# Loading the first piece of a transposed input whole, and rotating a projection's output tiles through eight PSUM banks instead of four

## The chip, the core and the metric

The kernel runs on one core of a Trainium2 chip. The metric is the device time of one execution in microseconds (us), as the median of several runs. Everything said below of the hardware comes from the profile of one execution and its trace.

## The reference

Two attention blocks read the same input `x` (1 x 2048 x 1024, bf16) and a gate mixes their results. Block A is linear attention, block B a sliding, dilated window of 8 keys. Cut to what matters here:

```python
def _A_ref(x, wqkv, wo):
    # H = 32 heads of Dh = 32
    q, k, v = qkv[0], qkv[1], qkv[2]                 # of x @ wqkv
    phi = lambda t: jnp.where(t > 0, t + 1, jnp.exp(t)) + 1e-6
    pq, pk = phi(q), phi(k)
    kv = jnp.einsum("bhsd,bhse->bhde", pk, v)
    z = jnp.einsum("bhsd->bhd", pk)
    num = jnp.einsum("bhqd,bhde->bhqe", pq, kv)
    den = jnp.einsum("bhqd,bhd->bhq", pq, z)[..., None] + 1e-6
    return (num / den) @ wo

g = _sigmoid((x * gate_w).sum(-1, keepdims=True))
return g * _A_ref(...) + (1 - g) * _B_ref(...)       # B: softmax over 8 keys, dilation 2
```

The change lies in the first stage only, which computes `pk = phi(x @ Wk)` of block A.

## The kernel before

The kernel is one long sequence of matrix products on TensorE (PE), with the order of PE's instructions written out by hand. Its stages are: A's key projection (`pk`, line 159), the products `G = x^T pk` (line 209) with sums and the gate's dot products beside them, small per-head products, the projections of B's values and A's queries (lines 284 and 320), B's windowed attention (lines 377 and 434 to 457), and the output projections (line 575).

In the first stage `x` is cut into 16 tiles of 128 rows (`t` from 0 to 15) and the 1024 output columns into two halves of 512. One output tile is 128 x 512 in f32 and fills one PSUM bank; eight matmuls, one for each block `kt` of 128 input columns, add up in it. The stationary operand is a 128 x 128 block of `x` transposed (`xT`), which DMA transposes bring in from memory. These all go out from the queue of SyncE (SP), mixed with plain loads of the weights.

The stage starts before `x` is there. So the first eight row tiles of half 0 are computed with the loop over `kt` outside: in four phases `k` of two `kt` each, every phase needs a quarter of the weight half `WkA0` (line 98) and two transposed pieces of `x` (line 94), for rows 0 to 511 and rows 512 to 1023. In phase 0 alone the first of these two pieces is issued in two halves. The quarter of the weights for phase 0 goes out from the queue of ScalarE (ACT), everything else from SP. After these pieces SP issues the row tiles 8 to 15, one transpose each (line 104), then the second weight half `WkA1` and the loads for the later stages (lines 81 and 89). While the first piece is on its way, PE runs 38 small matmuls on a constant (`warm_up`, line 165).

The eight open output tiles of the first eight rows use all eight PSUM banks: tiles 0 to 3 the pool `ps_pj` (tag `pj`, four banks), tiles 4 to 7 the pool `ps_1` (tag `p1`, four banks). All later tiles (8 to 15 of half 0, then 0 to 15 of half 1) take `ps_pj` alone, in turn. A tile gets a bank when the bank's tile before it has been read for the last time.

The function `phi` empties a bank in three steps: ACT writes `e = exp(pj)` (line 145), VectorE (DVE) takes `min(e, 1) + 1e-6` (line 146), and DVE writes `pk = max(pj, 0) + e` (line 147), which is the last reader of the bank. DVE's order in this stage is written out too: it goes from tile to tile.

GpSimd (POOL) builds a mask for block B in the meantime, with 72 selects (line 125) that nothing in this stage needs.

Of the kernel before, what the change touches and what calls it, by code (L numbers as in the profile page):

```python
# [11 lines left out]
F32 = mybir.dt.float32  # L12
# [3 lines left out]
P = 128  # L16
# [23 lines left out]
def kernel(  # L40
# [18 lines left out]
    def rows(ap, s0, s1):  # L59
        return ap[s0 // 1024, s0 % 1024:(s1 - 1) % 1024 + 1, :]  # L60
# [13 lines left out]
    ps_pj = ctx.enter_context(tc.tile_pool(name="ps_pj", bufs=4, space=bass.MemoryType.PSUM))  # L74
# [18 lines left out]
    def load_xT(k, t0, t1):  # L93
        nc.sync.dma_start_transpose(out=xT[:, 2 * k:2 * k + 2, t0 * P:t1 * P],  # L94
                                    in_=rows(x, t0 * P, t1 * P)[:, 2 * k * P:(2 * k + 2) * P])

    for k in range(4):
        (nc.sync if k else nc.scalar).dma_start(  # L98
            out=WkA[0][:, 2 * k:2 * k + 2, :],
            in_=A_wqkv[2 * k * P:(2 * k + 2) * P, D:D + 512].rearrange("(kt p) n -> p kt n", p=P))  # L100
        for t0, t1 in ((0, 4), (4, 8)) if k else ((0, 2), (2, 4), (4, 8)):
            load_xT(k, t0, t1)
    for t in range(8, NB):
        nc.sync.dma_start_transpose(out=xT[:, :, t * P:(t + 1) * P], in_=rows(x, t * P, (t + 1) * P))
    WkA += load_w("WkA", A_wqkv, D, "wa", only=(1,))
# [37 lines left out]
    def phi(work, dst, pj):  # L143
        e = work.tile([P, 512], F32, name="e", tag="e")
        nc.scalar.activation(out=e[:], in_=pj[:], func=ACT.Exp)  # L145
        nc.vector.tensor_scalar(out=e[:], in0=e[:], scalar1=1.0, scalar2=1e-6, op0=ALU.min, op1=ALU.add)  # L146
        nc.vector.scalar_tensor_tensor(out=dst, in0=pj[:], scalar=0.0, in1=e[:], op0=ALU.max, op1=ALU.add)  # L147

    with tc.manual_schedule(engines={PE}):

        with ExitStack() as s1:
            ps_1 = s1.enter_context(tc.tile_pool(name="ps_1", bufs=4, space=bass.MemoryType.PSUM))
# [5 lines left out]
            def project(pj, t, kt, half):  # L158
                nc.tensor.matmul(pj[:], lhsT=xT[:, kt, t * P:(t + 1) * P], rhs=WkA[half][:, kt, :],  # L159
                                 start=(kt == 0), stop=(kt == KT - 1))  # L160

            def warm_up(n):
                warm = ps_1.tile([P, P], F32, name="warm", tag="p1")
                for i in range(n):
                    nc.tensor.matmul(warm[:], lhsT=onesb[:], rhs=onesb[:], start=True, stop=True)


            warm_up(38)
            first = [(ps_pj.tile([P, 512], F32, name="pk_ps", tag="pj") if t < 4 else
                      ps_1.tile([P, 512], F32, name="pk1_ps", tag="p1")) for t in range(8)]  # L170
            for k in range(4):
                for t in range(8):
                    for kt in (2 * k, 2 * k + 1):
# [3 lines left out]
            for half in range(2):  # L177
                for t in range(NB):
                    if half == 0 and t < 8:
                        continue  # L180
                    pj = ps_pj.tile([P, 512], F32, name="pk_ps", tag="pj")
                    for kt in range(KT):
                        project(pj, t, kt, half)
                    phi(work, pk[:, t, half * 512:(half + 1) * 512], pj)
# [18 lines left out]
            for half in range(2):  # L203
                g_ = junk.tile([P, KT, 512], BF16, name=f"G{half}", tag=f"G{half}")
                G.append(g_)
                for kt in range(KT):
                    pj = ps_pj.tile([P, 512], F32, name="g_ps", tag="pj")
# [142 lines left out]
        with ExitStack() as s2:  # L350
# [159 lines left out]
            for c in range(KT):  # L510
                kts[c] = kpool.tile([P, 2, 1024], BF16, name="kt", tag="kt")
                for hh in range(2):
# [3 lines left out]
                    if 1 <= c <= 2:  # L516
                        t = 2 * (c - 1) + hh
# [28 lines left out]
        with ExitStack() as s3:  # L546
# [15 lines left out]
            def out_part(i, tb, c0, n):  # L562

                st = {}

                def mm(side, c):
                    if side == 0 and c == 0:
                        st["ps"] = ps_3.tile([P, 512], F32, name="e3_ps", tag="p3") if i % 2 else \
                            ps_pj.tile([P, 512], F32, name="d3_ps", tag="pj")
                    if side == 0:  # L570
                        lhsT, W = (pqT[0][:, c, tb * P:(tb + 1) * P] if tb < 4 else
                                   pqT[1][:, c, (tb - 4) * P:(tb - 3) * P]), WoA
                    else:
                        lhsT, W = OBT[:, c, tb * P:(tb + 1) * P], WoB
                    nc.tensor.matmul(st["ps"][:, 0:n], lhsT=lhsT, rhs=W[c0 // 512][:, c, c0 % 512:c0 % 512 + n],  # L575
                                     start=(side == 0 and c == 0), stop=(side == 1 and c == KT - 1))
                    if side == 0 or c < KT - 1:
                        return
                    osb = work3.tile([P, 512], BF16, name="osb", tag="e")
                    nc.scalar.activation(out=osb[:, 0:n], in_=st["ps"][:, 0:n], func=ACT.Copy,  # L580
                                         scale=omg[:, tb:tb + 1])
                    nc.scalar.dma_start(out=rows(out2, tb * P, (tb + 1) * P)[:, c0:c0 + n], in_=osb[:, 0:n])

                def side(k):
                    for c in range(KT):
                        mm(k, c)
                return side
# [3 lines left out]
            first = [out_part(i, *p_) for i, p_ in enumerate(parts[:7])]  # L591
# [42 lines left out]
```

## Time and profile before

| | us |
|---|---|
| median of three runs | 478.88 (478.12 to 479.05) |
| profiled execution, its own time | 478.26 |
| its span, first to last instruction | 476.5 |
| PE busy in the span | 468.6 (98%) |
| DVE busy | 278.2 (58%) |
| ACT busy | 168.6 (35%) |
| matmuls of the first stage (line 159), 256 of them | 56.6 busy, 3.8 idle before them |

An engine's busy time is the time in which it had an instruction at work. A line of the profile names source line, engine, operation, and the tiles written and read. "Idle before" is the time in which the engine had nothing to do just before an instruction of that group, and the arrow names what ended the wait. The operations on SP are the issues of DMAs: their time is that of the issue, not of the transfer. The granted clock of PE was 1.00 in all slices of the span.

### The profile page before, as it was taken

The page shows a single profiled execution, that of the slowest core. Times are in us where ns is not written, and L with a number is a line of the kernel's source. Part 1 is how long each engine was busy: PE and PEld are TensorE (multiplying, and loading weights), DVE is VectorE, ACT ScalarE, POOL GpSimd, SP SyncE. Part 2 cuts the span into 40 slices and gives each one's busy share as a digit, 9 for nine tenths or more (in the row PEclk, how much of TensorE's full clock was granted, in tenths as well). Part 3 has the DMA queues.
Part 4 walks back from the last instruction along what each step waited for, and adds up shares of the span by engine and source line. Part 5 has one row for each costly group of instructions (what it writes and reads, how often), then busy time and mean ns, then how long its engine had stood idle before and what let it go on. Part 6 is the DMA issues. An engine that isn't in the chain of part 4 may idle for free.

```text
span 476.5 us, 13198 instructions
## 1 busy us (share of the span) xinstructions
PE 468.6 (98%) x5750; PEld 244.3 (51%) x5750; DVE 278.2 (58%) x601; ACT 168.6 (35%) x271; POOL 24.5 (5%) x88
## 2 busy tenths in 40 slices
PE   8989999999999999999999999999999999999997
PEld 4334444444444444445666666666664444444444
DVE  0396679992228999999666676667670039800000
ACT  1243321111443333332546464646461134212121
POOL 3900000500000000001000000000000000000000
PEclk9999999999999999999999999999999999999999
DMA  7999990000635243627326545442452753221101
GB/s 164 179 254 377 348 291 1 0 1 0 200 94 151 79 142 121 170 77 256 105 60 102 74 95 86 95 88 66 86 149 72 161 150 78 68 55 42 38 33 45
DMA packets 98589, 55.41 MB, mean 116 GB/s; under 512 B 69858, under 2 KB 90466, under 8 KB 98530
## 3 DMA queue, kind: packets, MB, share of 16 engines
q1 hardware_dynamic: 93506, 50.10, 42.0%
q10 hardware_dynamic: 5024, 4.46, 2.8%
q8 instruction: 45, 0.74, 0.7%
q14 instruction: 14, 0.11, 0.1%
HBM read 26.10 MB, written 15.86 MB: 88 GB/s over the span
## 4 chain that ended last, share of the span: by engine, by line
PE 93%; SPq 2%; DVE 2%; DMA 1%; ACT 0%; issue 0%
PE q_ps L377 26%; PE d_ps L575 12%; PE p_ps L284 12%; PE g_ps L209 12%; PE e_ps L575 11%; PE p_ps L320 9%; PE pk_ps L159 7%; SPq L94 2%; PE o L457 2%; PE s2b L434 2%; DVE pk L147 1%; DMA xT<-in_A_x_dram 1%; DVE e L146 1%; PE kv_ps L229 0%; SPq L98 0%; PE w_ps L272 0%
## 5 line engine op out<-in xcount | busy, mean ns | idle before, releaser
L377 PE MATMUL q_ps<-xT,WqB 64*64 64x512 bf16 x1024 | 68.3, 377 | 0.0
L377 PE MATMUL q_ps<-xT,WkB 64*64 64x512 bf16 x1024 | 67.9, 376 | 0.0
L146 DVE TENSOR_SCALAR e<-e 128x512 f32<-128x512 f32 x64 | 28.4, 444 | 66.8 <-ACT e L145 66.7
L159 PE MATMUL pk_ps<-WkA,xT 128*128 128x512 bf16 x256 | 56.6, 379 | 3.8 <-DMA xT<-in_A_x_dram 2.0
L284 PE MATMUL p_ps<-WvB,xT 128*128 128x512 bf16 x256 | 57.9, 379 | 0.0
L209 PE MATMUL g_ps<-pk,xrow 128*128 128x512 bf16 x256 | 55.4, 379 | 0.0
L439 ACT ACTIVATE PT<-s2b 128x928 bf16<-128x928 f32 (+4 forms) x40 | 34.1, 854 | 46.1 <-PE s2b L434 46.1
L441 DVE TENSOR_TENSOR PT<-PT,mask 128x928 bf16<-128x928 bf16 (+4 forms) x40 | 23.6, 589 | 37.0 <-ACT PT L439 37.0
L320 PE MATMUL p_ps<-WqA,xT 128*128 128x512 bf16 x192 | 43.4, 379 | 0.0
L159 PEld LDWEIGHTS <-xT 128*128 128x128 bf16 x256 | 24.5, 98 | 35.6 <-DMA xT<-in_A_x_dram 5.6
L575 PEld LDWEIGHTS <-pqT 128*128 128x128 bf16 x264 | 25.7, 98 | 29.8 <-issue 0.4
L575 PEld LDWEIGHTS <-OBT 128*128 128x128 bf16 x264 | 25.8, 98 | 29.4
L209 PEld LDWEIGHTS <-xrow 128*128 128x128 bf16 x256 | 25.0, 98 | 30.2
L284 PEld LDWEIGHTS <-xT 128*128 128x128 bf16 x256 | 24.7, 98 | 30.0 <-issue 0.9
L377 PEld LDWEIGHTS <-WkB 64*64 64x64 bf16 x1024 | 32.1, 107 | 15.2 <-issue 0.6
L377 PEld LDWEIGHTS <-WqB 64*64 64x64 bf16 x1024 | 31.6, 107 | 15.3 <-issue 0.7
L145 ACT ACTIVATE e<-pk_ps 128x512 f32<-128x512 f32 x32 | 18.9, 597 | 44.8 <-PE pk_ps L159 39.5
L289 ACT CAST tmp<-p_ps 128x512 bf16<-128x512 f32 x32 | 18.7, 589 | 37.6 <-PE p_ps L284 32.3
L575 PE MATMUL d_ps<-WoA,pqT 128*128 128x512 bf16 (+1 forms) x136 | 31.3, 373 | 0.0
L575 PE MATMUL d_ps<-WoB,OBT 128*128 128x512 bf16 (+1 forms) x136 | 31.3, 373 | 0.0
L320 PEld LDWEIGHTS <-xT 128*128 128x128 bf16 x192 | 18.8, 98 | 22.6
L575 PE MATMUL e_ps<-WoA,pqT 128*128 128x512 bf16 (+1 forms) x128 | 29.4, 372 | 0.0
(62 smaller groups left out, 492.2 us busy)
## 6 DMA issues: line engine op xcount, KB each, us to landing
vd<-tmp SPq DMA_DIRECT2D x16, 264.0 KB
xrow<-in_A_x_dram SPq DMA_DIRECT2D x4, 1024.0 KB
out_dram<-osb ACTq DMA_DIRECT2D x31, 128.0 KB
pqd<-tmp SPq DMA_DIRECT2D x12, 256.0 KB
WvA<-in_A_wqkv_dram SPq DMA_DIRECT2D x2, 1024.0 KB
WoA<-in_A_wo_dram SPq DMA_DIRECT2D x2, 1024.0 KB
WvB<-in_B_wqkv_dram SPq DMA_DIRECT2D x2, 1024.0 KB
WqA<-in_A_wqkv_dram SPq DMA_DIRECT2D x2, 1024.0 KB
```

What stands on the lines that cost most here:

```text
L94: nc.sync.dma_start_transpose(out=xT[:, 2 * k:2 * k + 2, t0 * P:t1 * P], in_=rows(x, t0 * P, t1 * P)[:, 2 * k * P:(2 * k + 2) * P])
L145: nc.scalar.activation(out=e[:], in_=pj[:], func=ACT.Exp)
L146: nc.vector.tensor_scalar(out=e[:], in0=e[:], scalar1=1.0, scalar2=1e-6, op0=ALU.min, op1=ALU.add)
L159: nc.tensor.matmul(pj[:], lhsT=xT[:, kt, t * P:(t + 1) * P], rhs=WkA[half][:, kt, :], start=(kt == 0), stop=(kt == KT - 1))
L209: nc.tensor.matmul(pj[:], lhsT=xrow[:, t, kt * P:(kt + 1) * P], rhs=pk[:, t, half * 512:(half + 1) * 512], start=(t == 0), stop=(t == NB - 1))
L284: nc.tensor.matmul(st["pj"][:], lhsT=xT[:, kt, t * P:(t + 1) * P], rhs=WvB[half][:, kt, :], start=(kt == 0), stop=(kt == KT - 1))
L289: nc.scalar.copy(out=v[:, half * 16:(half + 1) * 16, 0:Dh], in_=st["pj"][:].rearrange("p (h e) -> p h e", h=16))
L320: nc.tensor.matmul(st["pj"][:], lhsT=xT[:, kt, t * P:(t + 1) * P], rhs=WqA[half][:, kt, :], start=(kt == 0), stop=(kt == KT - 1))
L377: nc.tensor.matmul(banks[o][64 * j:64 * j + 64, :], lhsT=lhsT(r, kt, j), rhs=rhs(r, kt), start=first and kt == 0, stop=kt == KT - 1, skip_ ...
L439: nc.scalar.activation(out=pt[:, :, 0:W_], in_=s2b[:].rearrange("p a b s -> p (a b) s")[:, :, 0:W_], func=ACT.Exp, scale=SCALE)
L441: nc.vector.tensor_tensor(out=pt[:, :, 0:W_], in0=pt[:, :, 0:W_], in1=mask[:, None, base:base + W_].broadcast_to([P, 4, W_]), op=ALU.mult)
L575: nc.tensor.matmul(st["ps"][:, 0:n], lhsT=lhsT, rhs=W[c0 // 512][:, c, c0 % 512:c0 % 512 + n], start=(side == 0 and c == 0), stop=(side == ...
```

## The change

It has two parts. First, phase 0 loads its first piece of `x` (rows 0 to 511) with one transpose instead of two, as the other phases do, so SP issues one DMA fewer. Second, every tile of the key projection takes its bank by its number: tiles 0 to 3 and 8 to 11 from `ps_pj`, tiles 4 to 7 and 12 to 15 from `ps_1`, in both halves. The order of the instructions on PE, ACT, DVE and POOL is as before; on SP it is as before without the one transpose.

```diff
-        for t0, t1 in ((0, 4), (4, 8)) if k else ((0, 2), (2, 4), (4, 8)):
-            load_xT(k, t0, t1)
+        for t in (0, 4):
+            load_xT(k, t, t + 4)
...
-            first = [(ps_pj.tile([P, 512], F32, name="pk_ps", tag="pj") if t < 4 else
-                      ps_1.tile([P, 512], F32, name="pk1_ps", tag="p1")) for t in range(8)]
+
+            def bank_k(t):
+                return (ps_1.tile([P, 512], F32, name="pk1_ps", tag="p1") if t & 4 else
+                        ps_pj.tile([P, 512], F32, name="pk_ps", tag="pj"))
+
+            first = [bank_k(t) for t in range(8)]
...
-                    pj = ps_pj.tile([P, 512], F32, name="pk_ps", tag="pj")
+                    pj = bank_k(t)
```

## The prediction

> **What bounds the kernel now.** The page's table of busy time comes first: PE is busy 98% of the span, so only PE's idle time can be won. Its groups put 3.8 us of that ahead of the matmuls of line 159, the stage that the change touches. The rest of the reading is where these lie. PE's timeline of the first 80 us (start, length, what; in brackets the idle time before it and what ended it):
>
> ```profile
> 4.80 4.14 PE L159 MATMUL pk_ps<-WkA,xT 128*128 128x512 bf16 x16
> 9.90 3.63 PE L159 MATMUL pk_ps<-WkA,xT 128*128 128x512 bf16 x16 [0.97 <-DMA xT<-in_A_x_dram]
> 14.05 3.63 PE L159 MATMUL pk_ps<-WkA,xT 128*128 128x512 bf16 x16 [0.52 <-DMA xT<-in_A_x_dram]
> 18.19 10.78 PE L159 MATMUL pk_ps<-WkA,xT 128*128 128x512 bf16 x48 [0.52 <-DMA xT<-in_A_x_dram]
> 30.48 34.69 PE L159 MATMUL pk_ps<-WkA,xT 128*128 128x512 bf16 x160 [1.51 <-DVE pk L147]
> ```
>
> The reader sees two limits. Phases 1 to 3 each start on a piece of xT. Then 48 matmuls run on (phase 3 and tiles 8 to 11), and tile 12 waits for DVE. From 30.48 us the 160 matmuls run at 34.69/160 = 0.2168 us each without a gap, and the chain of waits stays on PE.
>
> The queue of SP shows why the pieces come when they do:
>
> ```profile
> 0.80 3.94 SPq L94 DMA_TRANSPOSE xT<-in_A_x_dram  x3
> 4.79 0.58 SPq L98 DMA_DIRECT2D WkA<-in_A_wqkv_dram  x1
> 5.42 3.12 SPq L94 DMA_TRANSPOSE xT<-in_A_x_dram  x2
> 8.59 0.58 SPq L98 DMA_DIRECT2D WkA<-in_A_wqkv_dram  x1
> 9.22 3.19 SPq L94 DMA_TRANSPOSE xT<-in_A_x_dram  x2
> ```
>
> It issues without a pause. The three first transposes start at 0.80, 2.16 and 3.44, and take 1.30, 1.24 and 1.30 us, though the first two move half as much. The windows then tell whether the DMA engines keep up (last columns: clock, mean busy share of the DMA engines, GB/s):
>
> ```profile
> 2.00:7.00 5.00, 4.85 (x40) 3.22 (x37) 0.00 (x0) 0.08 (x1) 0.00 (x0) 1.00 0.73 174
> 7.00:18.00 11.00, 9.15 (x40) 3.66 (x40) 0.00 (x0) 0.00 (x0) 8.62 (x47) 1.00 1.15 197
> 18.00:30.00 12.00, 10.69 (x48) 4.61 (x49) 10.23 (x18) 6.29 (x11) 5.60 (x30) 1.00 1.18 176
> ```
>
> Up to 7 us they have idle time (0.73), after that they are full, and single issues stretch to 1.8 to 2.1 us. DVE's part, from the chain of waits:
>
> ```profile
> 18.83 0.60 ACT e L145
> ...
> 19.46 1.68 DVE e L146
> ...
> 21.16 0.69 DVE pk L147
> 21.85 0.40 DVE e L146
> ...
> 29.74 0.70 DVE pk L147
> 30.44 0.04 issue
> 30.48 34.69 PE pk_ps L159 x160
> ```
>
> DVE takes 0.69 + 0.34 + 0.02 = 1.06 us a tile and works off a backlog of eight tiles, finished by phase 3 at 0.43 us a tile. Its ninth, tile 8, ends at 30.44 and frees tile 12's bank. The first DVE step took 1.68 us where later ones take 0.42.
>
> **What the Trainium skill says.** "Perfetto Trace Analysis", section Matmuls: independent matmul groups should rotate through different PSUM banks so that emptying one overlaps the next group. The trace agrees: the rotation over four banks ends in the wait above. The same page, DMA Instruction — HWDGE: the profiled time of a DMA issue is descriptor generation, not the movement. The trace agrees: equal issue times for 128 and 256 KB. "SBUF — State Buffer", section Who interferes with whom: a DVE instruction in a two-port mode, such as tensor_scalar, and a GpSimd instruction exclude each other. The trace agrees in kind: POOL's 72 selects of line 125 run from 9.20 to about 23.1 us, and the DVE step of 1.68 us (line 146) is a tensor_scalar that began amid them.
>
> **Part 1, one transpose fewer.** The second issue and its gap go: 3.44 - 2.16 = 1.28 us. Every later DMA of SP (the piece for rows 512 to 1023, nine more issues of phases 1 to 3, tiles 8 to 15, WkA1, the rows of x) may go out up to 1.28 us earlier. That is the upper bound, since the windows show room: the 0.73 x 5 us of work up to 7 us would fit into 3.2 us at 1.15. For the lower bound I take the DMA engines as one server, starting at 2.1 us, where the first issue ends: 0.71 us for a weight quarter (256 KB at 367 GB/s, the rate of the window 30 to 45), 1.43 us for a 256 KB transpose (between 176 and 197 GB/s). Before: quarter and first half done at 3.53, second half 4.25, third piece (issued by 4.74) 6.17. After: quarter and whole piece 4.24, next 5.67. So 0.5 us. I take **0.9 us**.
>
> The first matmul loses something. The pieces landed 3.95, 3.77 and 3.59 us after their issues began (PE's waits ended at 4.79 or before, 5.93 and 7.03). The whole piece lands at 0.80 + 3.6 = 4.4 to 0.80 + 3.95 + 0.74 (128 KB more at 176 GB/s) = 5.5 us, against 4.79. Phase 0 then ends by 5.5 + 16 x 0.2168 = 9.0 at the latest, and its second piece (2.16 + 3.6 = 5.8) is no longer waited for. Phase 1 cannot start before 9.90 - 0.9 = 9.0 anyway. So this costs nothing; what covers it is the wait of 0.97 us ahead of phase 1. If that cover were gone, up to 0.7 us would show. Phases 1, 2 and 3 start 0.9 us earlier.
>
> Then tile 8. It started at 21.89, waiting for both its own xT (issued at 15.93) and bank 0, which DVE left at 21.16 + 0.69 = 21.85. Phase 3 had ended by 21.7. So DVE's first tile must move as well. ACT's exp does, with phase 3. The DVE step behind it then meets POOL's selects at 18.6 instead of 19.46, and POOL does not move. The trace shows this once: 1.25 us lost, while two more steps amid the selects took 0.47. The bounds: no loss at all (tile 8 then starts 0.2 us earlier still, at the end of phase 3), or held until the selects end (rival 2). I take the 1.25 us again: tile 8 starts at 21.0. A like delay of the second step would cost tile 9 at most 1.25 - (1.73 - 1.06) = 0.6.
>
> **Part 2, eight banks.** Tile 12 could start 32 x 0.2168 = 6.94 us after tile 8, at 28.83; it starts at 30.48. The **1.65 us** between go (the timeline's 1.51 counts from the end of the last matmul, which outlasts its slot). After the change tile 12 waits for DVE's tile 4, which ended at 26.20: 2.6 us to spare, more for each tile after it, since PE takes 1.73 us a tile and DVE 1.06. Late next would be data: tile 11, issued at 21.52, was used by 27.1 without a wait, so a transpose takes at most 5.6 us there, and tile 12 (issued 22.88) is there by 28.5. WkA1, issued 28.66, is first needed at 37.4 and then at 34.9; from 31 us on the rate is that of plain loads (over 310 GB/s), so its 1 MB is there at about 33.8, less what part 1 gives. No other instruction is added, and the one DMA wait removed (PE's for rows 256 to 511) lay inside phase 0.
>
> Downstream the stage G at 65.2 us follows PE; its rows of x have long landed, and each later load that waits for PE moves with it. Nothing I found in the page's chain is paced by anything but PE after 30.48.
>
> **Sum.** 1.65 + 0.9 = 2.55 us: the profiled execution goes from 478.26 (span 476.5 and 1.76 around it) to 475.7. That execution lies 0.62 below the median of 478.88, so the time to compare is 478.88 - 2.55 = **476.3**.
>
> **Rivals.**
> 1. *POOL's lock swallows part 1.* If DVE gets the port at a fixed point of POOL's sequence (21.14 - 0.42 = 20.7 us), tile 8 stays at 21.89 and only 1.65 is won: 477.2. For: POOL's selects run back to back, without regard to DVE. Against: the later steps got in at once. 28%.
> 2. *DVE is held until the selects end.* The step then starts at about 22.7 and bank 0 is free at 22.7 + 0.42 + 0.69 = 23.8, 1.95 later than now; less 1.65: 479.2. 7%.
> 3. *Slower: the transposes stream worse.* Fuller earlier, the DMA engines might serve the pieces at a lower rate (197 fell to 176 GB/s as it is). It decides once phase 3 or tile 8 is so late that tile 8 starts after 21.89 + 1.65 + 0.96 = 24.5, 13% more for the 20 us of streaming: 480 or more. Against: same bytes, and pieces of a form that phases 1 to 3 already use. 4%.
> 4. *The bank was not what tile 12 waited for.* If its xT landed only at 30.4, the pools bring nothing: 478.0. For: PE's weight load for tile 12 also started only then. Against: the estimate of 28.5 above. 6%.
>
> **Numbers.** The forecast itself has 55%: 475.9 to 476.7 from part 1's bounds. With 0.5 us for the spread of runs (478.12 to 479.05) and rival 1, the range is 475.4 to 477.9. A difference of 0.2%, 0.96 us, is about what can be told from no change. Faster: 55 + 28 + half of rival 4 = 86%; the same 10%; slower 4%.
>
> **What would show it.** Right: SP's second weight load issued at 3.5 instead of 4.79; phase 1's matmuls at about 9.0; no wait for DVE near 29, the matmuls of line 159 running on from tile 8 to the end of the stage, and line 209 starting at 62.6 instead of 65.2. Part 1 is wrong if phase 3 still starts at 18.2, or if tile 8 waits for DVE near 21.9; part 2 is wrong if a wait of over 0.5 us remains between tiles 8 and 15 or ahead of half 1.

## The result, and the profile after

The changed kernel takes 475.02 us (median of four runs, 474.26 to 475.77) against 478.50 us for the kernel before: 3.5 us less, a ratio of 0.9927 with a 95% interval of 0.9906 to 0.9947. The prediction was 476.3 with a range of 475.4 to 477.9. The direction was right; the gain of 2.55 us was too small, and 475.02 lies below the range.

PE's timeline of the first stage in the changed kernel (start, length, what; in brackets the idle time before and what ended it):

```profile
5.80 14.00 PE L159 MATMUL pk_ps<-WkA,xT 128*128 128x512 bf16 x62 [0.45 <-DMA xT<-in_A_x_dram]
20.29 41.61 PE L159 MATMUL pk_ps<-WkA,xT 128*128 128x512 bf16 x189 [0.48 <-DMA xT<-in_A_x_dram]
```

Two rows are left where there were five. The four phases run from 5.80 to 19.8 us as one block, then PE waits 0.48 us for tile 8's piece of `x`, and from 20.29 us it runs to the end of the stage. The wait for DVE ahead of tile 12 is gone. (A few matmul records are missing from this trace, hence the counts of 62 and 189 for 64 and 192.) The next stage's first matmul of line 209 before, now line 213, starts at 61.74 us against 65.01: 3.27 us. These are the lines of before and after:

```profile
65.01 55.42 PE L209 MATMUL g_ps<-pk,xrow 128*128 128x512 bf16 x256
61.74 55.20 PE L213 MATMUL g_ps<-pk,xrow 128*128 128x512 bf16 x250
```

Tile 8 gives 21.89 - 20.29 = 1.60 of these, the bank 1.65.

SP's queue in the changed kernel:

```profile
0.80 2.83 SPq L94 DMA_TRANSPOSE xT<-in_A_x_dram  x2
3.67 0.58 SPq L98 DMA_DIRECT2D WkA<-in_A_wqkv_dram  x1
4.31 3.04 SPq L94 DMA_TRANSPOSE xT<-in_A_x_dram  x2
...
14.62 1.41 SPq L104 DMA_TRANSPOSE xT<-in_A_x_dram  x1
```

The second weight load goes out at 3.67 instead of 4.79, and tile 8's transpose at 14.62 instead of 15.93, so the whole issue time saved, 1.1 to 1.3 us, came through in this pair of profiles. The windows say that the DMA engines took it (last columns: clock, busy share of the DMA engines, GB/s):

```profile
2.00:7.00 5.00, 4.55 (x38) 3.69 (x36) 0.00 (x0) 0.08 (x1) 0.00 (x0) 1.00 0.95 210
7.00:18.00 11.00, 10.95 (x52) 4.90 (x51) 0.52 (x2) 1.18 (x3) 7.19 (x38) 1.00 1.11 219
```

Up to 7 us their share is 0.95 instead of 0.73, and the rate rises in both windows. DVE's first steps in the changed kernel:

```profile
17.45 0.48 DVE L146 TENSOR_SCALAR e<-e 128x512 f32<-128x512 f32 x1 [16.39 <-ACT e L145]
17.96 0.69 DVE L147 SCALAR_TENSOR_TENSOR pk<-pk_ps,e 128x512 bf16<-128x512 f32 x1
18.57 0.42 DVE L146 TENSOR_SCALAR e<-e 128x512 f32<-128x512 f32 x1
```

The first step takes 0.48 us, where it took 1.67 in the profiled execution before. It comes amid POOL's selects all the same, which run from 10.68 to 25.71 us here (before: from 9.20). The prediction had this step lose 1.25 us again, and POOL not move.

The profiled execution, 475.77 us, is the slowest of the four. Its span fell by 2.5 us and not by 3.27: from 352.95 us PE stood 0.54 us in line 461 waiting for nothing that the profile shows. A later profile of the same kernel (474.09 us) has no such pause.

### The profile page after: what moved, and what is told of

It reads as the page before. It is cut to its first block, busy times and chain, and to the rows that moved or that the text cites. A ratio compares the mean times of both kernels' runs of the same rounds, so it can differ in the third digit from the quotient of the medians.

```text
span 474.0 us, 13165 instructions
## 1 busy us (share of the span) xinstructions
PE 466.4 (98%) x5718; PEld 245.7 (52%) x5750; DVE 277.1 (58%) x601; ACT 168.7 (36%) x271; POOL 25.5 (5%) x88
## 4 chain that ended last, share of the span: by engine, by line
PE 95%; SPq 3%; DMA 1%; issue 1%; ACT 0%
PE q_ps L381 26%; PE d_ps L579 12%; PE p_ps L288 12%; PE g_ps L213 12%; PE e_ps L579 11%; PE pk_ps L159 9%; PE p_ps L324 9%; SPq L94 2%; PE o L461 2%; PE s2b L438 2%; DMA xT<-in_A_x_dram 1%; PE kv_ps L233 0%; SPq L98 0%; PE w_ps L276 0%; ACT osb L584 0%
## 5 line engine op out<-in xcount | busy, mean ns | idle before, releaser
L146 DVE TENSOR_SCALAR e<-e 128x512 f32<-128x512 f32 x64 | 27.4, 428 | 64.9 <-ACT e L145 64.9
L159 PE MATMUL pk_ps<-WkA,xT 128*128 128x512 bf16 x251 | 55.4, 379 | 1.2 <-DMA xT<-in_A_x_dram 0.9
L584 ACT ACTIVATE osb<-d_ps,omg 128x512 bf16<-128x512 f32 (+1 forms) x17 | 11.5, 674 | 50.1 <-PE d_ps L579 48.4
```

## The experiments

The theory after the result was that the two parts do not add. What starts DVE earlier also shortens the wait for a bank, and POOL's hold on DVE's first step (the step gets no further while the selects run) is paid twice in the kernel before: ahead of tile 8 and ahead of tile 12. The rival was the prediction's sum of two independent parts.

**One part at a time, and the issue count alone.**

```diff
 # part1_only: kernel before, with
-        for t0, t1 in ((0, 4), (4, 8)) if k else ((0, 2), (2, 4), (4, 8)):
+        for t0, t1 in ((0, 4), (4, 8)):
```

> The first piece of x whole, all later tiles on ps_pj as before the change. Theory (the two parts overlap: what starts DVE earlier also shortens the wait for a bank): as in the changed kernel, tile 8 starts near 20.3 us and the first DVE step takes about 0.45 us; DVE then leaves tile 8 near 27.4, when tile 12 could start at 20.3 + 6.94 = 27.2, so the wait for DVE shrinks from 1.65 to about 0.2 us and this part alone brings about 3.0 us. Rival (the parts add, as the prediction had it): the bank still costs 1.65 us, and this part alone brings 1.6 us.

Measured: 474.85 us (474.70 to 475.19) against 478.43 on the same chip, ratio 0.9939 (0.9914 to 0.9965). PE's timeline:

```profile
5.39 14.36 PE L159 MATMUL pk_ps<-WkA,xT 128*128 128x512 bf16 x64
20.08 7.08 PE L159 MATMUL pk_ps<-WkA,xT 128*128 128x512 bf16 x32 [0.32 <-DVE e L146]
27.37 34.69 PE L159 MATMUL pk_ps<-WkA,xT 128*128 128x512 bf16 x160 [0.21 <-DVE pk L147]
```

Four banks, and the wait ahead of tile 12 is 0.21 us instead of 1.51. Line 209 starts at 61.90 us against 65.01, 3.1 us earlier, as the theory had it (3.0). In the medians part 1 alone brings 3.6 us, and not the rival's 1.6.

```diff
 # part2_only: changed kernel, with the load loop of the kernel before
-        for t in (0, 4):
-            load_xT(k, t, t + 4)
+        for t0, t1 in ((0, 4), (4, 8)) if k else ((0, 2), (2, 4), (4, 8)):
+            load_xT(k, t0, t1)
```

> Banks by tile number, the first piece of x still in two halves. Theory: tile 8 stays near 21.9 (or 21.5 where DVE's first step is not held), the wait ahead of tile 12 goes, and 1.65 us is won (up to 2.0). Rival (tile 12 was waiting for its piece of x and not for a bank): under 0.3 us.

Measured: 476.83 us (475.29 to 477.23), ratio 0.9978 (0.9965 to 0.9992): 1.6 us, as expected. Alone, the parts bring 3.6 and 1.6 us; together 3.5 to 3.9. So the two gains don't add: once part 1 is there, little is left of the bank's 1.65 us. The times lie in two groups: 19 of the 22 took 476.56 to 477.23 us and three 475.29 to 475.63. More banks alone do not take the upper group away; with part 1 alone all seven executions lie within 0.5 us.

```diff
 # split_second: changed kernel, with
-        for t in (0, 4):
-            load_xT(k, t, t + 4)
+        for t0, t1 in ((0, 4), (4, 8)) if k else ((0, 4), (4, 6), (6, 8)):
+            load_xT(k, t0, t1)
```

> The changed kernel, with the second piece of phase 0 (rows 512 to 1023) issued in two halves instead of the first: the first piece is whole, but SP issues as many DMAs as before the change. Theory (part 1 works by SP's issue time): the second weight load goes out at 4.8 us and tile 8's transpose at 15.9, as before the change, tile 8 starts at 21.5 to 21.9, and of the 3.3 us only 1.65 to 2.0 are left. Rival (a larger first transfer keeps the DMA engines better fed): tile 8 starts near 20.3 and the full 3.3 us stay.

Measured: 475.72 us (475.12 to 477.23), ratio 0.9959 (0.9940 to 0.9978). PE's timeline up to tile 8:

```profile
9.13 3.63 PE L159 MATMUL pk_ps<-WkA,xT 128*128 128x512 bf16 x16 [0.31 <-DMA xT<-in_A_x_dram]
13.17 3.63 PE L159 MATMUL pk_ps<-WkA,xT 128*128 128x512 bf16 x16 [0.41 <-DMA xT<-in_A_x_dram]
17.13 3.63 PE L159 MATMUL pk_ps<-WkA,xT 128*128 128x512 bf16 x16 [0.33 <-DMA xT<-in_A_x_dram]
20.98 13.99 PE L159 MATMUL pk_ps<-WkA,xT 128*128 128x512 bf16 x64 [0.22 <-DMA xT<-in_A_x_dram]
```

With one issue more, the waits ahead of phases 1 to 3 and of tile 8 are back, 1.27 us in all. That fits the issue count, but does not prove it: part2_only has as many issues, and in its profile only 0.20 us of such waits. The loss is 0.9 us against part 1 alone, and neither expectation fits: most of part 1's gain survives. Two of its 12 executions, at 476.91 and 477.23 us, lie above the other ten (up to 476.23). In the profiled execution DVE's first step took 0.55 us. That pointed at POOL's hold as the larger share of the gain.

**POOL's hold.**

```diff
 # before_no_selects: kernel before, without the 72 selects
-    for half in range(2):
...
-                nc.gpsimd.affine_select(out=dst, in_=dst, compare_op=ALU.is_ge, fill=0.0, base=base,
-                                        pattern=[[sign, w]], channel_multiplier=-sign)
```

> The kernel before the change without POOL's 72 selects, so the window mask of block B is all ones. Theory (POOL held DVE's first step for 1.25 us, and DVE held tile 8 and tile 12): the first DVE step takes about 0.42 us, DVE leaves tile 0 near 20.6, tile 8 starts when its xT lands (21.5 if it takes 5.6 us from its issue, as in the changed kernel), tile 12 waits until DVE leaves tile 8 near 29.1 and starts 1.35 us earlier than before: about 1.3 us won without any change to loads or banks. Rival (tile 8 waits for its xT until 21.85, and the hold on DVE only filled that time): tile 8 stays at 21.9, tile 12 starts at 29.1 all the same, as DVE's chain is what frees it; then the gain is also about 1.3 us but no part of it at tile 8. Second rival (the hold is not POOL's): the first DVE step still takes 1.7 us and nothing changes.

Measured: 475.75 us (475.17 to 476.63), ratio 0.9958 (0.9943 to 0.9973). With loads and banks untouched, taking POOL's selects out brings 2.7 us, twice what was expected. The first step took 0.43 us. In this execution tile 12 did not wait for a bank at all, but half 1 waited 0.77 us for the second weight half at 35.7 us.

The times of the kernel before lie in two groups. Of the 103 executions of it that ran beside these kernels, 80 took 477.95 to 478.94 us and 23 took 475.5 to 476.9; the four ahead of the result were all in the upper one. Without the selects only the lower group is left.

```diff
 # before_pool_late: kernel before, with
-    nc.gpsimd.memset(mask[:], 1.0)
+    for _ in range(4):
+        nc.gpsimd.memset(mask[:], 1.0)
```

> The kernel before the change with POOL writing the mask's ones four times instead of once, which puts off its 72 selects by about 2.9 us; nothing else is changed, and the selects still run while DVE begins. Theory (the hold depends on how far POOL's selects have run when DVE's first step comes: about 57 of 72 in the held execution, 37 to 49 in those that were not held): the first step comes at about the 40th select and is not held, the upper group of times (478.3 to 478.9) is gone, and the median is about 475.8, as without the selects. Rival (any select at work can hold it): two thirds of the executions stay near 478.5.

Measured: 476.18 us (475.56 to 476.64) against 478.22, ratio 0.9962 (0.9948 to 0.9977). All 72 selects are there, only later, and in eight executions the upper group is gone. The wait ahead of tile 12 is 0.76 us here, half of what it was, with the same four banks. DVE's first step and POOL's selects of this kernel, from its timeline:

```profile
18.36 0.43 DVE L147 TENSOR_SCALAR e<-e 128x512 f32<-128x512 f32 x1 [17.30 <-ACT e L146]
...
12.81 15.28 POOL L126 TENSOR_SCALAR_AFFINE_SELECT mask<-mask 64x64 bf16<-64x64 bf16 x72 [7.61 <-issue]
```

The kernel before was then profiled twice more, unchanged.

> The kernel before the change once more, for a second profile. Theory (two groups of times, set by whether POOL holds DVE's first step): if its time lies at 478.3 or above, the first step of line 146 takes 1.5 us or more and comes near 19.4 us; if at 476.9 or below, it takes about 0.45 us, comes near 18.4, and the wait ahead of tile 12 is about 0.8 us. Rival (the groups come from something later in the program): the first step is the same in both.

> As before_b: a third profile of the kernel before the change, to see one execution of the lower group of times.

Measured: 478.45 and 478.06 us, both in the upper group. The lower group of this kernel was not caught in a profile; that its step is not held is inferred, from the two runs above and from the profile of part2_only, an execution of the lower group with a first step of 0.47 us. DVE, POOL and PE of the first:

```profile
18.32 2.73 DVE L146 TENSOR_SCALAR e<-e 128x512 f32<-128x512 f32 x1 [17.26 <-ACT e L145]
...
9.30 14.06 POOL L125 TENSOR_SCALAR_AFFINE_SELECT mask<-mask 64x64 bf16<-64x64 bf16 x72 [7.48 <-issue]
...
21.83 7.07 PE L159 MATMUL pk_ps<-WkA,xT 128*128 128x512 bf16 x32 [1.15 <-DVE pk L147]
30.40 34.69 PE L159 MATMUL pk_ps<-WkA,xT 128*128 128x512 bf16 x157 [1.50 <-DVE pk L147]
```

Here the step came at 18.32, more than a microsecond before the one shown in the prediction, and still ended at 21.05 (there 21.13). It is the end that is fixed, not the loss. And here tile 8 plainly waits for DVE, 1.15 us; in the first profile the same start was put down to a DMA.

The traces give the starts that this explains. In the three profiles of the kernel before, phase 3 began at 18.19, 17.05 and 17.33 us, but tile 8 at 21.89, 21.83 and 21.70: tile 8 did not follow the phases, it followed the end of the hold. In the kernels with the same loads whose step was not held (part2_only, before_no_selects, before_pool_late) phase 3 began at 16.85 to 17.09 and tile 8 at 20.58 to 20.67.

POOL's selects show the hold from their side (before_b, then part2_only):

```profile
20.62 0.52 POOL L125 TENSOR_SCALAR_AFFINE_SELECT mask<-mask 64x57 bf16<-64x57 bf16 x1
18.22 0.45 POOL L125 TENSOR_SCALAR_AFFINE_SELECT mask<-mask 64x56 bf16<-64x56 bf16 x1
```

In before_b the selects from the 39th to the 61st start about every 0.18 us, and their lengths grow from 0.24 to 0.30 us. The 62nd takes 0.52, DVE's step ends within it, and the next select is back at 0.23. In part2_only DVE got in during the 48th. In all four held profiles the long select is the 61st to 63rd of the 72.

**The changed kernel again, with POOL and DVE shifted.**

> The changed kernel as it is, to have its times beside those of the others. Theory (part 1 takes DVE's first step out of POOL's hold, so all executions lie in one group): 474.3 to 475.8 throughout, about 475.0 in the middle. Rival (the hold only became rarer): some executions 1.5 to 2.5 us above that.

Measured: 474.33 us (474.09 to 474.57) against 478.22, ratio 0.9927 (0.9911 to 0.9944): one group. PE's timeline shows a single block of matmuls from 5.50 us to the end of the stage, and line 213 starts at 60.76.

```diff
 # after_no_selects: changed kernel, without the 72 selects
-    for half in range(2):
...
-                nc.gpsimd.affine_select(out=dst, in_=dst, compare_op=ALU.is_ge, fill=0.0, base=base,
-                                        pattern=[[sign, w]], channel_multiplier=-sign)
```

> The changed kernel without POOL's 72 selects, so block B's mask is all ones. Theory (after the change POOL costs nothing any more, as tile 8 waits for its xT and the banks come free early enough): same as the changed kernel within 0.3 us. Rival (part 1 only hides part of POOL's cost): up to 0.8 us faster.

Measured: 474.55 us (474.26 to 474.84), the same as the changed kernel beside it. After the change POOL costs nothing.

```diff
 # after_dve_late: changed kernel, with (after_dve_mid: range(16))
+            idle = junk.tile([P, D], F32, name="idle", tag="zacc")
+            for i in range(17):
+                nc.vector.memset(idle[:], float(i))
```

> The changed kernel with 17 fills of an unused tile (128 x 1024 f32, about 1.1 us each) on DVE ahead of its first tile, so that DVE's first step of line 146 comes at about 19.9 us instead of 17.4, when POOL is at about its 55th select. Theory (a first step that comes late in the run of selects is held): it takes 1 us or more instead of 0.44, as in the held execution of the kernel before. Rival (the hold has nothing to do with how far the selects are): 0.42 to 0.55 us. The time itself is later than the changed kernel's by what DVE comes late, 1 to 2.5 us, and tells little; the length of the step decides.

Measured: 478.48 us (476.88 to 480.36). The eleven executions from 478.42 us up had a mean granted clock of PE of 0.995 or 0.996, the nine others (476.88 to 477.65) 0.999 or 1.000. The fills took 1.19 us each with their gaps, so the step came at 21.12, 11.4 us after the first select, and took 0.37 us. By then the hold would have been over; this execution tells nothing on it.

> As after_dve_late with 16 fills instead of 17, so that DVE's first step comes at about 19.9 us, 9.3 to 10.3 us after POOL's selects began. Theory (a first step that comes between about 8.9 and 11.3 us after the selects began is held until 11.3 to 11.5, whatever the loads and the banks do): in the changed kernel too it takes 1.3 to 2.3 us and ends 11.7 to 11.9 us after the first select, tile 8 starts near 22, about 476.5. Rival (only the kernel before the change is held, so the cause lies in its loads or its banks): 0.42 to 0.55 us, tile 8 near 21.1, about 475.3.

Measured: median 475.79, but spread over 475.69 to 480.16. In the profiled execution (477.05 us):

```profile
19.93 1.61 DVE L146 TENSOR_SCALAR e<-e 128x512 f32<-128x512 f32 x1
...
9.96 14.07 POOL L125 TENSOR_SCALAR_AFFINE_SELECT mask<-mask 64x64 bf16<-64x64 bf16 x72 [8.15 <-issue]
```

The step is held in the changed kernel too, and ends 11.58 us after the first select. So the hold is not tied to the loads or the banks. But 11 of the 20 executions took 475.69 to 475.84 us, near what the rival had for a step that is not held, and seven took 478.5 or more, which neither theory expected. Those seven had a mean granted clock of 0.993 or 0.996, the 13 others 0.999 or 1.000. A clock 0.4% lower stretches 476 us by 1.9 us (an estimate), so the clock accounts for most of what they took beyond 475.7. Only the two kernels with fills show it; why isn't shown. At the full clock two of 13 executions, the profiled one among them, lie 1.2 to 1.6 us above the rest. The profiles of all kernels with selects, side by side:

| kernel | first select | DVE's first step | after the select | it took |
|---|---|---|---|---|
| before_pool_late | 12.81 | 18.36 | 5.55 | 0.43 |
| changed | 10.68 | 17.45 | 6.77 | 0.48 |
| after_again | 10.11 | 17.13 | 7.02 | 0.44 |
| part1_only | 9.68 | 17.40 | 7.72 | 0.43 |
| whole_late | 9.85 | 17.80 | 7.95 | 0.52 |
| part2_only (475.29 us, the lower end) | 9.40 | 18.11 | 8.71 | 0.47 |
| split_second | 9.60 | 18.40 | 8.80 | 0.55 |
| before_b | 9.30 | 18.32 | 9.02 | 2.73 |
| before_c | 9.17 | 18.60 | 9.43 | 2.32 |
| after_dve_mid | 9.96 | 19.93 | 9.97 | 1.61 |
| before | 9.20 | 19.46 | 10.26 | 1.67 |
| after_dve_late | 9.73 | 21.12 | 11.39 | 0.37 |

In these twelve executions a step that came up to 8.8 us after the first select lost at most 0.13 us; one that came from 9.0 to 10.3 us after it was held until its end fell 11.6 to 11.9 us after it; one that came 11.4 us after it lost nothing. The line at about 8.9 us is read off the profiles, one of each kernel but three of the kernel before; what draws it stays open.

**A version that might beat both.**

```diff
 # whole_late: changed kernel, with
-        for t in (0, 4):
-            load_xT(k, t, t + 4)
+        for t0, t1 in ((0, 4), (4, 8)) if k < 2 else ((0, 8),):
+            load_xT(k, t0, t1)
```

> The changed kernel with phases 2 and 3 loading their pieces of x by one transpose for all 1024 rows, so SP issues two DMAs fewer. In the changed kernel PE runs phases 0 to 3 without a gap and waits only 0.45 us for the first piece and 0.48 us for tile 8's. Theory (SP's issue time still sets when tile 8's transpose starts): tile 8's piece is issued up to 2.6 us earlier, the 0.48 us go, 474.5. Rival (the DMA engines are full by then, share 1.1): the issues of double size take twice as long or wait, tile 8 starts at 20.3 as before, and a piece that lands later may even cost PE up to 1 us: 475 to 476.

Measured: 474.92 us (474.53 to 475.02), 0.6 us slower than the changed kernel beside it. The issue for 1024 rows took 3.52 us in phase 2, and PE waited for its piece:

```profile
13.07 48.52 PE L159 MATMUL pk_ps<-WkA,xT 128*128 128x512 bf16 x220 [0.76 <-DMA xT<-in_A_x_dram]
```

The rival was right about the wait; the time lies just under its 475. No version with all 72 selects beats the changed kernel: this one and part 1 alone come closest, with ratios of 0.9938 and 0.9939 against 0.9927 and intervals that overlap.

## Why the prediction fell short

- **"I take the 1.25 us again: tile 8 starts at 21.0": the step that failed.** The hold was taken as a length that moves along with the phases. It is an end, at a place in POOL's selects, and a step that comes early enough escapes it. In the changed kernel the hold fell to 0.06 us, DVE left tile 0 at 18.65, and tile 8 waited for its own xT until 20.24: it started at 20.29, 1.60 us earlier and not 0.9. Rival 1 had the fixed end right, at 20.7 us in POOL's sequence, but not that the step could slip in ahead of it. By the table above, the step at 18.6 that the prediction expected, 9.4 us after the first select at 9.20, would have been held, and tile 8 would have stayed near 21.8, as in rival 1. It came at 17.45, 8.3 us after 9.20, and POOL began later as well, at 10.68; why it did isn't shown. Rival 2, held until the selects end, did not happen.
- **Part 1's 0.9 us: too small as well.** Of the bounds 0.5 and 1.28 the upper one held for the issues: tile 8's transpose went out 1.31 us earlier. The lower bound, from the DMA engines as one server at a fixed rate, was too low: the profiled execution showed 210 and 219 GB/s. The phases came earlier by more than the upper bound: phase 3 began at 16.18 instead of 18.19. The 18.19 was itself late: the other profiles with three issues for phase 0's pieces have 16.85 to 17.33, those with two 15.87 to 16.54. Of the 2.0 us some 0.9 therefore lay in the one profile that was read. Phase 3 ended at 19.8, and so the bound "no loss at all", tile 8 at the end of phase 3 (20.8), was passed too. Behind a step at 17.45 even another 1.25 us would have freed bank 0 by 19.9, ahead of tile 8's xT. So the 21.0 missed by two errors, the hold as a length and the phases' shift, and no run tells what each is worth.
- **The bank ahead of tile 12, 1.65 us: right in size, half right in cause.** The wait is gone in the changed kernel, and the banks alone brought 1.6 us, upper group against upper group. But the stall was priced as a lack of banks only. It was as much DVE's chain beginning late: with four banks the wait is 0.76 us once the selects come later, and 0.21 with part 1. The three executions of part2_only in the lower group lie only 0.3 us below the lower group of the kernel before. So the parts overlap, and the sum treated them as independent. That nothing is late next in its place was right for the changed kernel. The weight half WkA1 was put at 33.8 us too early: half 1 waited for it at 35.4 us in split_second and at 35.7 us in before_no_selects.
- **The spread.** The three runs ahead of the prediction were all of the upper group. Against its lower group (median 475.9) the changed kernel gains some 0.9 to 1.6 us, taking its medians of 475.02 and 474.33. The range had no case for the groups.
- Phase 0's cover held: the first matmul came at 5.80 instead of 4.80, later than the 5.5 estimated, and no phase after it waited. One reading was off without effect: line 209 began at 65.01 us before the change, where the prediction has 65.2.

## What to carry to other kernels

Price a stall by everything that stands behind it: a wait for a buffer can be the late start of the engine that empties it, and then an earlier start and more buffers are two cures for one wait, not two gains. Where one instruction of a group takes a multiple of the others, find out whether its length or its end is fixed before it is carried over, for a second profile of the same kernel tells this at once. Look at the single times for groups, not only at the median.

## What the runs showed of the hardware

A DVE tensor_scalar (128 x 512, f32) beside POOL's back-to-back selects of 0.22 to 0.31 us each was not held for one select but for up to 2.3 us (2.73 less 0.42), through a dozen of them. Without the selects the same step took 0.43 us. The Trainium skill ("SBUF — State Buffer", Who interferes with whom) has the loser wait for the whole instruction of the other, which here would be about 0.3 us; the measurement decides. And at the head of SP's queue a piece of `x` of 256 KB took the same 1.3 us to issue (1.30 and 1.34) as one of 128 KB (1.30 and 1.24), while one of 512 KB, further back in the queue, took 2.3 to 3.5 us.
